# Dense layer with Mish on one core: x tiles 0 and 1 loaded as two, k 0 of w1 as two, and the first block multiplied in another order

## The chip, the core and the metric

The kernel runs on one core of one Trainium2 chip. A core has TensorE (PE), which multiplies and writes to PSUM; VectorE (DVE), ScalarE (ACT) and GpSimd (POOL), which work element by element; and SyncE (SP), which here only issues DMAs. Each engine takes its own instructions in order and waits for the others by semaphores. The metric is the device time of one execution in microseconds, as the median of several runs.

## The reference

x is 2048 x 512 (one batch), w1 512 x 1792, b1 1792 long, w2 1792 x 512, all bf16.

```python
def reference(x, w1, b1, w2):
    h = jnp.einsum("bsd,df->bsf", x, w1) + b1
    sp = jnp.log1p(jnp.exp(-jnp.abs(h))) + jnp.where(h > 0, h, jnp.zeros_like(h))
    act = h * jnp.tanh(sp)
    return jnp.einsum("bsf,fd->bsd", act, w2)
```

The function between the two products is Mish.

## The kernel before

The contraction over D = 512 has four k tiles of 128, F = 1792 has fourteen f tiles of 128, and S = 2048 is cut into four blocks of 512 rows, each of four row tiles of 128. A block takes two stages. In the first (line 180) each of its fourteen f tiles gets four matmuls, one for each k, with w1 as the weights and the transposed x (xT) as the moving operand, 512 columns wide; they add up in one of the eight PSUM banks. ScalarE reads the bank, adds the bias, applies Mish and writes bf16 to a_sb (line 163). In the second stage (line 202) each row tile gets fourteen matmuls, one for each f, with a_sb as the weights and w2 as the moving operand; VectorE copies the result to o_sb (line 208) and SP stores it. The fourteen f of a block take 56 matmuls of 512 columns, and so does its second stage.

x is needed transposed. Blocks 1 to 3 and row tiles 2 and 3 of block 0 are transposed by DMA. Row tiles 0 and 1 come as they are (x_nat) and are transposed by TensorE: sixteen small matmuls against an identity (line 147), each of half a tile's rows, into PSUM, from where VectorE and ScalarE copy them to xT (line 155). Until x_nat is there, TensorE runs a fill of matmuls on constants (line 105, WARM), whose results nobody reads.

Nothing schedules this program: the order of every engine is the order in which the code is written, and a wait is on the instruction that first needs it. The DMAs stand in two queues. ACT's queue gets k 0 and k 2 of w1 for f tiles 0 to 7. SP's queue gets x_nat, k 1, then, behind a wait for the third fill matmul, the DMA transpose of tiles 2 and 3, then k 3, the bias, the rest of w1 (f 8 to 13, all k), w2, and the transposes of blocks 1 to 3.

In block 0 the eight f tiles 0 to 7 are open at once, one PSUM bank each, and the calls of `first(fs, js, ks)` walk over them by k and by row tile: a call issues for every k and f one matmul over the row tiles js. The banks of f 0 to 7 are also those that the transposes of x used (line 147), so the first matmul into a bank waits until its transposes have been copied out. Each row tile is one fourth of a bank's columns, so a matmul over one tile has 128 columns, over two 256, over four 512. With the last k of an f its Mish is issued. f tiles 8 to 13 follow one by one with 512 columns (`mm1`).

## Time and profile before

| | us | |
|---|---|---|
| median of 3 runs | 105.19 | 105.11 to 105.49 |
| span of the profiled execution | 102.9 | first to last instruction |
| TensorE busy | 100.2 | 97% of the span |
| ScalarE busy | 39.5 | 38% |
| VectorE busy | 13.1 | 13% |
| chain: line 180 and line 202 | | 47% each |
| chain: the fill, line 105 | | 3% |

For the profiled execution the page gives the span alone. The median is 2.3 us above it; what lies outside the span (before the first instruction and after the last) is in no row.

How to read what follows. Times in a row are microseconds from the start of the span, engines as above; PEld is TensorE's loading of weights, which runs beside its matmuls, and SPq or ACTq an instruction that issues a DMA on that engine. A row of the timeline has the start, how long it lasted, engine, line, operation, what is written from what, the shape and how many were merged; in brackets the idle time before it and who ended it. Matmuls are pipelined: the time of one reaches into the next, so a pace is read from starts, not from durations. In rows the weights w1 and w2 are both called w_sb, and b1_sb is b_sb.

### The profile page before, as it was taken

To read this page: it belongs to the slowest core of one execution; us is meant where nothing else is said; L and a number is where in the kernel's file an instruction comes from. 1 tells how busy PE (TensorE), PEld (TensorE's weight loads), DVE (VectorE), ACT (ScalarE), POOL (GpSimd) and SP (SyncE) were. 2 spreads that over 40 slices of the span, in tenths; PEclk is the share of its full clock that TensorE was granted. 3 is DMA by queue.
4 is the path that set the end of the run, shared out by engine and by line. 5 is a ranking of instruction groups with operands and counts; after the bars stand their busy time and mean duration, and the time that the engine had idled before them with its cause. 6 is when DMAs were issued, how large, how long until landed. Compare 5 with 4: busy or idle time off the path is not lost.

```text
span 102.9 us, 1196 instructions
## 1 busy us (share of the span) xinstructions
PE 100.2 (97%) x527; PEld 48.8 (47%) x527; DVE 13.1 (13%) x26; ACT 39.5 (38%) x61; POOL 0.4 (0%) x5
## 2 busy tenths in 40 slices
PE   6999999999999999999999999999999999999993
PEld 2697444444444444444444444444444444444472
DVE  1203000220220000022220000022201000020241
ACT  4301999000047777000017777400006777700000
POOL 1000000000000000000000000000000000000000
DMA  2999999991110000011001000001111000001112
GB/s 61 375 283 358 363 243 112 269 237 51 51 51 0 0 6 0 0 51 51 20 31 51 0 0 10 0 3 48 51 51 51 0 0 0 0 6 51 51 51 51
DMA packets 12977, 7.94 MB, mean 77 GB/s; under 512 B 7980, under 2 KB 12332, under 8 KB 12972
## 3 DMA queue, kind: packets, MB, share of 16 engines
q1 hardware_dynamic: 12540, 7.33, 27.4%
q10 hardware_dynamic: 432, 0.54, 1.5%
q8 instruction: 4, 0.07, 0.3%
q14 instruction: 1, 0.01, 0.0%
HBM read 3.94 MB, written 2.10 MB: 59 GB/s over the span
## 4 chain that ended last, share of the span: by engine, by line
PE 97%; DVE 0%; ACT 0%; issue 0%
PE ps L180 47%; PE ps L202 47%; PE ps L105 3%; DVE xT L155 0%; ACT o_sb L232 0%; PE ps L147 0%
## 5 line engine op out<-in xcount | busy, mean ns | idle before, releaser
L163 ACT ACTIVATE a_sb<-ps,b_sb 128x512 bf16<-128x512 f32 x56 | 37.1, 698 | 47.9 <-PE ps L180 47.9
L180 PE MATMUL ps<-xT,w_sb 128*128 128x512 bf16 (+2 forms) x252 | 49.1, 355 | 0.2 <-DVE xT L155 0.2
L202 PE MATMUL ps<-w_sb,a_sb 128*128 128x512 bf16 (+3 forms) x252 | 49.1, 355 | 0.0
L180 PEld LDWEIGHTS ps<-xT,w_sb 128*128 128x128 bf16 x252 | 24.2, 98 | 24.1 <-DVE xT L155 0.3
L202 PEld LDWEIGHTS ps<-w_sb,a_sb 128*128 128x128 bf16 x252 | 23.2, 98 | 25.5
L208 DVE CAST o_sb<-ps 128x512 bf16<-128x512 f32 x15 | 10.4, 692 | 79.8 <-PE ps L202 79.8
L232 ACT ACTIVATE o_sb<-ps 128x64 bf16<-128x64 f32 x1 | 0.2, 224 | 11.5 <-PE ps L202 11.5
L105 PE MATMUL ps<-const-bfloat16-1.0 128*128 128x512 bf16 (+1 forms) x7 | 2.7, 566 | 0.8 <-PEq L289 0.8
L105 PEld LDWEIGHTS ps<-const-bfloat16-1.0 128*128 128x128 bf16 x7 | 0.9, 138 | 2.1 <-issue 2.1
L155 ACT ACTIVATE xT<-ps 128x256 bf16<-128x256 f32 (+1 forms) x3 | 0.9, 347 | 1.7 <-PE ps L147 1.7
L107 ACT ACT_TABLE_LOAD x1 | 1.3, 1283 | 0.7 <-PEq L289 0.7
L250 DVE STREAM_TRANSPOSE b_T<-b_nat 32x32 bf16<-32x32 bf16 x4 | 0.8, 202 | 3.3 <-DMA b_nat<-in_b_dram 3.2
L232 DVE CAST o_sb<-ps 128x320 bf16<-128x320 f32 (+1 forms) x2 | 0.8, 392 | 1.5 <-PE ps L202 1.5
L155 DVE CAST xT<-ps 128x128 bf16<-128x128 f32 (+1 forms) x2 | 0.6, 354 | 2.4 <-PE ps L147 2.4
L147 PEld LDWEIGHTS ps<-ident,x_nat 64*128 64x128 bf16 x16 | 0.4, 118 | 0.4 <-DMA x_nat<-in_x_dram 0.4
L147 PE MATMUL ps<-ident,x_nat 64*128 64x64 bf16 x16 | 0.5, 222 | 0.0
L130 DVE TENSOR_SCALAR ident<-diff 128x128 bf16<-128x128 int32 x1 | 0.2, 227 | 0.2 <-POOL diff L128 0.2
L128 POOL IOTA diff<- 128x128 int32 x1 | 0.2, 234 | 0.4 <-POOLq L289 0.4
L102 DVE MEMSET b_nat<- 32x64 uint32 x1 | 0.1, 112 | 0.8 <-PEq L289 0.8
L252 DVE CAST b_sb<-b_T 128x14 f32<-128x14 bf16 x1 | 0.2, 176 | 0.0
L289 POOL MEMSET const-bfloat16-1.0<- 128x1 bf16 x1 | 0.1, 102 | 0.0
L289 POOL MEMSET const-uint8-127<- 128x1 uint8 x1 | 0.1, 102 | 0.0
(2 smaller groups left out, 0.2 us busy)
## 6 DMA issues: line engine op xcount, KB each, us to landing
out_dram<-o_sb SPq DMA_DIRECT2D x15, 128.0 KB, 1.7
w_sb<-in_w_dram SPq DMA_DIRECT2D x1, 1792.0 KB, 10.7
w_sb<-in_w_dram SPq DMA_DIRECT2D x1, 768.0 KB, 6.1
w_sb<-in_w_dram ACTq DMA_DIRECT2D x2, 256.0 KB, 3.7
w_sb<-in_w_dram SPq DMA_DIRECT2D x2, 256.0 KB, 3.7
x_nat<-in_x_dram SPq DMA_DIRECT2D x1, 256.0 KB, 2.6
out_dram<-o_sb SPq DMA_DIRECT2D x1, 80.0 KB, 1.6
xT<-in_x_dram SPq DMA_TRANSPOSE x4, 5.0
```

Of the source, the lines that this page charges most:

```text
L105: t_fill = [pe.mark(nc.tensor.matmul(ps[:, 7, 0:n], c_w, c_m[:, 0:n], start=True, stop=True)) for n in WARM]
L107: act.eng.preload_act_table(ACT.Mish)
L128: t_diff = pool.mark(pool.eng.iota(diff[:, :], pattern=[[1, P]], base=0, channel_multiplier=-1))
L130: t_id = dve.mark(nc.vector.tensor_scalar(ident[:, :], diff[:, :], 0, None, ALU.is_equal))
L147: mm = nc.tensor.matmul(ps[:, b0 + h, lo:lo + H], x_nat[g, j, k * P:(k + 1) * P], ident[g, g], start=True, stop=True)
L155: t = eng.mark(nc.vector.tensor_copy(dst, src) if eng is dve else act.eng.activation(dst, src, ACT.Copy))
L163: t = act.mark(act.eng.activation(a_sb[:, f, starts[s]:starts[s + 1]], ps[:, bank, 0:n], ACT.Mish, bias=b1_sb[:, f:f + 1]))
L180: return nc.tensor.matmul(ps[:, bank, lo:hi], w1_sb[:, k, f * P:(f + 1) * P], xT[:, k, starts[s] + lo:starts[s] + hi], start=first, stop=( ...
L202: return nc.tensor.matmul(ps[:, bank, 0:hi - lo], a_sb[:, f, i * P:(i + 1) * P], w2_sb[:, f, lo:hi], start=(f == 0), stop=(f == FT - 1))
L208: t = dve.mark(nc.vector.tensor_copy(o_sb[:, i, lo:hi], ps[:, bank, 0:hi - lo]))
L232: t = eng.mark(nc.vector.tensor_copy(dst, src) if eng is dve else act.eng.activation(dst, src, ACT.Copy))
L250: t = dve.mark(nc.vector.transpose(b1_T[j * SQ:(j + 1) * SQ, :], b1_nat[:, j * SQ:(j + 1) * SQ]))
```

## The change

- Row tiles 0 and 1 of x are loaded as two DMAs of 128 KB, each with a semaphore of its own, a tile's 128 consecutive rows over the 128 partitions. Before, partition p held rows 2p and 2p + 1, and the output rows of the first two tiles were written back in that order; now they are written tile by tile.
- k 0 of w1 for f 0 to 7 comes as two DMAs of 128 KB, f 0 to 3 and f 4 to 7.
- k 3 of w1 stands ahead of the DMA transpose in SP's queue, and the transpose waits for the fourth fill matmul instead of the third.
- The fill has one 256-column matmul less.
- The transposes go tile by tile: for tile i its k 0 first, copied by VectorE, then k 1 to 3, copied by ScalarE in one instruction of 3 x 128 columns. Tile 0 uses banks 0, 1, 4, 5 and tile 1 banks 2, 3, 6, 7.
- In block 0, tiles 0 and 1 take all four k of f 0 to 7 first, with k 1 of f 0 to 3 ahead of k 0 of f 4 to 7; then tiles 2 and 3 take all four k of one f after the other, each with its Mish behind it.

```diff
-WARM = (512,) * 5 + (256,) * 2
+WARM = (512,) * 5 + (256,)
+HALF = 4
...
-        for k in (0, 2):
-            load_part(act, k, k + 1, 0, OPEN)
-        t_xn = load(sp, x_nat[:, :, :], x2[0:2 * P, :].rearrange("(p j) d -> p j d", p=P), "s_xn")
+        load_part(act, 0, 1, 0, HALF)
+        load_part(act, 0, 1, HALF, OPEN)
+        load_part(act, 2, 3, 0, OPEN)
+        t_xn = [load(sp, x_nat[:, i, :], x2[i * P:(i + 1) * P, :], "s_xn%d" % i) for i in range(2)]
         load_part(sp, 1, 2, 0, OPEN)
-        sp.wait(t_fill[2])
+        load_part(sp, 3, 4, 0, OPEN)
+        sp.wait(t_fill[3])
         t_x23 = load(sp, xT[:, :, 2 * P:4 * P], x2[2 * P:4 * P, :], "s_x23", True)
-        load_part(sp, 3, 4, 0, OPEN)
...
-            pe.wait(t_xn, t_id)
             H = P // 2
-            for b0, eng, js, ks in ((0, dve, (0,), (0,)), (2, act, (1,), (0,)), (4, dve, (0, 1), (1,)), (6, act, (0, 1), (2, 3))):
...
+            pe.wait(t_id)
+            for i in (0, 1):
+                pe.wait(t_xn[i])
+                for eng, b0, ks in ((dve, 2 * i, (0,)), (act, 4 + 2 * i, (1, 2, 3))):
...
+                    dst = xT[:, ks[0]:ks[-1] + 1, i * P:(i + 1) * P].rearrange("p k (h t) -> p k h t", h=2)
+                    src = ps[:, b0:b0 + 2, 0:m * H].rearrange("p h (k t) -> p k h t", k=m)
...
-            if i < 2:
-                return out2[0:2 * P, :].rearrange("(p j) d -> p j d", p=P)[:, i, :]
             return out2[i * P:(i + 1) * P, :]
...
-        first(range(4), (0,), (0,))
-        first(range(4), (1,), (0,))
-        first(range(4, OPEN), (0, 1), (0,))
-        first(range(OPEN), (0, 1), (1, 2))
-        first(range(OPEN), (2, 3), (0, 1, 2))
-        first(range(OPEN), None, (3,), True)
+        first(range(HALF), (0,), (0,))
+        first(range(HALF), (1,), (0,))
+        first(range(HALF), (0, 1), (1,))
+        first(range(HALF, OPEN), (0, 1), (0, 1))
+        first(range(OPEN), (0, 1), (2, 3))
+        for f in range(OPEN):
+            first((f,), (2, 3), range(KT), True)
```

TensorE's order from the transposes to the wait for tiles 2 and 3, before. c_dve and c_act are VectorE's and ScalarE's semaphores, s_xn the load of x_nat, s_w1_1_0 the load of k 1 from f 0 on, s_x23 the DMA transpose of tiles 2 and 3.

```order
L147 MATMUL ps<-ident,x_nat 128x64 [waits c_dve,s_xn]
L147 MATMUL ps<-ident,x_nat 128x64 x15
L180 MATMUL ps<-xT,w_sb 128x128 [waits s_w1_0_0,c_dve]
L180 MATMUL ps<-xT,w_sb 128x128
L180 MATMUL ps<-xT,w_sb 128x128 [waits c_act]
L180 MATMUL ps<-xT,w_sb 128x128 x5
L180 MATMUL ps<-xT,w_sb 128x256 [waits c_dve]
L180 MATMUL ps<-xT,w_sb 128x256
L180 MATMUL ps<-xT,w_sb 128x256 [waits c_act]
L180 MATMUL ps<-xT,w_sb 128x256
L180 MATMUL ps<-xT,w_sb 128x256 [waits s_w1_1_0]
```

And TensorE in the changed program at the same place, where s_xn0 and s_xn1 are the loads of tiles 0 and 1 and s_w1_0_4 that of the second half of k 0.

```order
L149 MATMUL ps<-ident,x_nat 128x64 [waits s_xn0,c_dve]
L149 MATMUL ps<-ident,x_nat 128x64 x7
L149 MATMUL ps<-ident,x_nat 128x64 [waits s_xn1]
L149 MATMUL ps<-ident,x_nat 128x64 x7
L181 MATMUL ps<-xT,w_sb 128x128 [waits s_w1_0_0,c_dve]
L181 MATMUL ps<-xT,w_sb 128x128
L181 MATMUL ps<-xT,w_sb 128x128 [waits c_dve]
L181 MATMUL ps<-xT,w_sb 128x128 x5
L181 MATMUL ps<-xT,w_sb 128x256 [waits c_act,s_w1_1_0]
L181 MATMUL ps<-xT,w_sb 128x256 x3
L181 MATMUL ps<-xT,w_sb 128x256 [waits s_w1_0_4]
```

The wait for k 1 moved from behind eight 128-column and four 256-column matmuls to behind the eight alone, and tile 1's transposes, with a wait of their own, stand ahead of the first matmul of line 181. The third 128-column matmul, into bank 2, waits for VectorE's copy of tile 1 where it waited for ScalarE's.

SP's queue at its start, before:

```order
L85 DMA x_nat<-in_x_dram 128x1024 [waits barrier_Pool_Activation_PE_DVE_SP_release]
L85 DMA w_sb<-in_w_dram 128x1024
L85 DMA_TRANSPOSE xT<-in_x_dram 128x4x256 [waits c_pe]
L85 DMA w_sb<-in_w_dram 128x1024
L85 DMA b_nat<-in_b_dram 14x128 [waits c_dve]
```

and SP's queue in the changed program:

```order
L86 DMA x_nat<-in_x_dram 128x512 [waits barrier_Pool_Activation_PE_DVE_SP_release]
L86 DMA x_nat<-in_x_dram 128x512
L86 DMA w_sb<-in_w_dram 128x1024 x2
L86 DMA_TRANSPOSE xT<-in_x_dram 128x4x256 [waits c_pe]
L86 DMA b_nat<-in_b_dram 14x128 [waits c_dve]
```

One DMA more stands ahead of k 1, and k 3 moved from behind the DMA transpose to ahead of it.

More of the change, by code (lines that the diff above doesn't have):

```diff
@@ L136, in transpose_x @@
         def transpose_x():
-            pe.wait(t_xn, t_id)
             H = P // 2
-            for b0, eng, js, ks in ((0, dve, (0,), (0,)), (2, act, (1,), (0,)), (4, dve, (0, 1), (1,)), (6, act, (0, 1), (2, 3))):
-                m = len(js)
-                for i, k in enumerate(ks):
-                    for n, j in enumerate(js):
-                        lo = (i * m + n) * H
+            pe.wait(t_id)
+            for i in (0, 1):
+                pe.wait(t_xn[i])
+                for eng, b0, ks in ((dve, 2 * i, (0,)), (act, 4 + 2 * i, (1, 2, 3))):
+                    m = len(ks)
+                    for n, k in enumerate(ks):
                         for h in (0, 1):
                             g = slice(h * H, (h + 1) * H)
-                            mm = nc.tensor.matmul(ps[:, b0 + h, lo:lo + H], x_nat[g, j, k * P:(k + 1) * P], ident[g, g],
-                                                  start=True, stop=True)
-                eng.wait(pe.mark(mm))
-                for i, k in enumerate(ks):
-                    dst = xT[:, k, js[0] * P:(js[-1] + 1) * P].rearrange("p (j h t) -> p j h t", j=m, h=2)
-                    src = ps[:, b0:b0 + 2, i * m * H:(i + 1) * m * H].rearrange("p h (j t) -> p j h t", j=m)
+                            mm = nc.tensor.matmul(ps[:, b0 + h, n * H:(n + 1) * H], x_nat[g, i, k * P:(k + 1) * P],
+                                                  ident[g, g], start=True, stop=True)
+                    eng.wait(pe.mark(mm))
+                    dst = xT[:, ks[0]:ks[-1] + 1, i * P:(i + 1) * P].rearrange("p k (h t) -> p k h t", h=2)
+                    src = ps[:, b0:b0 + 2, 0:m * H].rearrange("p h (k t) -> p k h t", k=m)
                     if m == 1:
@@ L155, in transpose_x @@
                     t = eng.mark(nc.vector.tensor_copy(dst, src) if eng is dve else act.eng.activation(dst, src, ACT.Copy))
-                    for j in js:
-                        t_cp[j, k] = t
-                free[b0] = free[b0 + 1] = [t]
+                    for k in ks:
+                        t_cp[i, k] = t
+                    free[b0] = free[b0 + 1] = [t]
         def mish(s, f, bank, t_mm):
```

## The prediction

> **What bounds the kernel now.** I read the chain of waits first, in order of time:
>
> ```profile
> 0.73 0.04 issue
> 0.77 2.72 PE ps L105 x7
> 3.49 0.19 PE ps L147 x3
> 3.68 0.02 issue
> 3.70 0.30 DVE xT L155
> 4.00 0.12 issue
> 4.13 12.32 PE ps L180 x84
> 16.45 12.09 PE ps L202 x56
> ```
>
> From 4.13 us on TensorE alone sets the time: every later piece is a run of matmuls that follows the one before without a gap. So the time can change in only three ways: by when the first matmul of line 180 starts, by gaps inside the first stage, and by the matmuls' own number and width. Their pace comes from the starts in the PE timeline, asked at narrow stretches:
>
> ```profile
> 4.13 0.22 PE L180 MATMUL ps<-xT,w_sb 128*128 128x128 bf16 x1 [0.17 <-DVE xT L155]
> ...
> 4.57 0.49 PE L180 MATMUL ps<-xT,w_sb 128*128 128x256 bf16 x3
> 5.01 0.49 PE L180 MATMUL ps<-xT,w_sb 128*128 128x256 bf16 x3
> 4.79 4.75 PE L180 MATMUL ps<-xT,w_sb 128*128 128x256 bf16 x42
> ...
> 16.28 0.38 PE L202 MATMUL ps<-w_sb,a_sb 128*128 128x512 bf16 x1
> ```
>
> Eight 128-column matmuls take 4.13 to 4.57, 0.055 us each. Four 256-column ones take 4.57 to 5.01, and 42 of them end 4.75 us after the first started: less the last one's own 0.27 that is 41 steps of 0.109. A 512-column one takes 12.09 / 56 = 0.216 (chain). Check: 5.01 + 40 x 0.1093 + 32 x 0.2159 = 16.29, and the second stage starts at 16.28. **The first stage has no gap once it runs**; at 5.01 it turns to k 1. The question is when the changed program gets there, and with how much work left.
>
> **The loads.** When they are issued (SP and ACT timelines), and how long until they land (the DMA view, asked around each issue):
>
> ```profile
> 0.74 0.40 SPq L85 DMA_DIRECT2D x_nat<-in_x_dram  x1
> ...
> 0.95 0.86 ACTq L85 DMA_DIRECT2D w_sb<-in_w_dram  x2
> ...
> 1.19 0.42 SPq L85 DMA_DIRECT2D w_sb<-in_w_dram  x1
> 2.24 1.31 SPq L85 DMA_TRANSPOSE xT<-in_x_dram  x1
> 3.60 0.57 SPq L85 DMA_DIRECT2D w_sb<-in_w_dram  x1
> 4.73 0.95 SPq L85 DMA_DIRECT2D w_sb<-in_w_dram  x2
> ...
> x_nat<-in_x_dram SPq DMA_DIRECT2D x1, 256.0 KB, 2.6
> w_sb<-in_w_dram ACTq DMA_DIRECT2D x1, 256.0 KB, 3.0
> w_sb<-in_w_dram ACTq DMA_DIRECT2D x2, 256.0 KB, 3.7
> w_sb<-in_w_dram SPq DMA_DIRECT2D x1, 256.0 KB, 3.6
> xT<-in_x_dram SPq DMA_TRANSPOSE x1, 4.4
> w_sb<-in_w_dram SPq DMA_DIRECT2D x1, 256.0 KB, 3.7
> w_sb<-in_w_dram SPq DMA_DIRECT2D x1, 768.0 KB, 6.1
> ```
>
> So x lands at 0.74 + 2.6 = 3.34, w1 k 0 at 3.95, k 1 at 1.19 + 3.6 = 4.79, x tiles 2-3 at 6.64, k 3 at 7.30, the rest of w1 at 10.83. ACT's two have a median of 3.7 and the first took 3.0, so k 2 (issued about 1.36) took some 4.4 and lands at about 5.8. The queue rows of three short stretches (2.45-2.70, 3.05-3.35, 3.65-3.95) show in what order the bytes move, q1 being SP's queue and q10 ACT's:
>
> ```profile
> q1 hardware_dynamic: 45, 0.09, 94.5%
> ...
> q10 hardware_dynamic: 56, 0.11, 98.4%
> ...
> q1 hardware_dynamic: 56, 0.11, 102.8%
> ```
>
> x alone, then k 0 alone, then k 1 alone: loads are served one after another in the order of issue, whichever queue they stand in. In the changed program that order is x0 (SP, 0.74), k 0 first half (ACT, 0.95), x1 (SP, about 1.19), k 0 second half (ACT, 1.36), k 1 (SP, about 1.64), k 2, k 3, x tiles 2-3. **Ahead of the end of k 1 stand the same 768 KB as before**, and no split can bring it forward.
>
> What the split costs is the rate. The windows view, whose last number is GB/s:
>
> ```profile
> 1.75:2.40 0.65, 0.65 (x3) 0.15 (x1) 0.00 (x0) 0.27 (x1) 0.00 (x0) 1.00 0.91 154
> 2.50:4.50 2.00, 1.83 (x27) 1.05 (x26) 0.62 (x2) 0.74 (x3) 0.00 (x0) 1.00 1.04 391
> 11.00:13.00 2.00, 2.00 (x11) 0.87 (x9) 0.00 (x0) 2.00 (x5) 0.00 (x0) 1.00 1.08 356
> ```
>
> Rows of 2048 bytes move at 391 GB/s (2.5 to 4.5); w2, with rows of 1024 bytes, at 356 (11 to 13). The 512 KB of x and k 0 now go in rows of 1024 bytes: 1.47 us for 1.34, so +0.13. The slow start (154 GB/s, 100 KB by 2.40) is either of bytes or of pieces; in the second case pieces of half the size leave 50 KB more to do, another 0.13. I take the first, as the rate is the only part that a row shows, and keep the second for the range.
>
> Landings after: x0 at 3.34 - 0.34 + 0.03 = 3.03; the first half of k 0 at 3.40; x1 at 3.95 - 0.37 + 0.10 = 3.68; the second half at 4.08; **k 1 at 4.79 + 0.13 = 4.92**.
>
> **TensorE's path after.** How long a landed x takes until it is multiplied:
>
> ```profile
> 3.42 0.13 PEld L147 LDWEIGHTS ps<-ident,x_nat 64*128 64x128 bf16 x4 [0.41 <-DMA x_nat<-in_x_dram]
> 3.70 0.29 DVE L155 CAST xT<-ps 128x128 bf16<-128x128 f32 x1 [2.38 <-PE ps L147]
> 4.10 0.18 PEld L180 LDWEIGHTS ps<-xT,w_sb 128*128 128x128 bf16 x3 [0.26 <-DVE xT L155]
> L155 ACT ACTIVATE xT<-ps x3: 278/378/384, 3.8 to 4.3; 128x256 bf16<-128x256 f32 x2, 128x128 bf16<-128x128 f32 x1
> L147 PEld LDWEIGHTS ps<-ident,x_nat x16: 95/124/129, 3.4 to 3.7; 64*128 64x128 bf16 x16
> ```
>
> Landing to weights 0.08, to the cast 0.36, to the matmul 4.13 - 3.34 = 0.79.
>
> - The fill is a 256-column matmul shorter and ends about 3.07; x0's transposes wait for x0 until 3.11, so that edit is hidden.
> - TensorE takes its instructions in order, so x1's transposes stand ahead of the first matmul: they wait until 3.76 and are through by about 3.96 (sixteen took 0.4, eight 0.2). The first matmul starts at about 3.99, where it was 4.13: 0.14 earlier.
> - Only f 0 and 1 can run: banks 2 and 3 held x1's transposes and are free with x1's VectorE cast, at 3.68 + 0.79 = 4.47. Six 128-column matmuls follow, to 4.80.
> - ACT now casts k 1-3 of a tile at once, 384 columns. 128 took 0.278 and 256 took 0.381, so 0.484 by the slope; the ends are 0.381 and 0.765, a narrower and two separate ones. After x1: 0.08, eight transposes and their end 0.4, the cast 0.48, 0.1 to the matmul: 3.68 + 1.07 = 4.75, at worst 5.03.
> - The next matmul is of k 1, which lands at 4.92 and is ready 0.11 later (0.08 as above, 0.03 from weights to matmul): **5.03**. This wait ends last. The four f of the second half of k 0 are queued behind it, though their weights are there.
>
> Now the work. Before, 40 of 256 and 32 of 512 columns were left at 5.01. After, only the eight 128-column matmuls are done, and 60 of 256 and 24 of 512 are left: 6.56 + 5.18 = 11.74. The first stage ends at 5.03 + 11.74 = 16.77 instead of 16.28, **+0.49 us**. Of it 0.44 is the work that before hid the wait for k 1 (four 256-column matmuls moved behind it), 0.02 that sixteen 256-column matmuls replace eight of 512, 0.02 the later turn to k 1; the rest is rounding.
>
> Later waits are covered. k 2 is wanted at 5.03 + 1.32 = 6.35 and lands at 5.9; k 3 at 7.22, and with it now ahead of the transpose it lands about 5.9 + 0.67 = 6.6. x tiles 2-3 are wanted at 8.10; everything up to k 3 landed at 7.30 before, so 7.43 after is its bound, a cover of 0.7. Each 0.1 beyond that costs 0.1. The rest of w1 is wanted at 8.10 + 32 x 0.109 = 11.6, against 10.96. SP's wait moves from the third to the fourth fill, 0.43 later, but two loads that stood behind the transpose are now one, so what follows on SP is issued no later. The bias and Mish:
>
> ```profile
> 8.44 0.18 DVE L252 CAST b_sb<-b_T 128x14 f32<-128x14 bf16 x1
> 9.86 8.21 ACT L163 ACTIVATE a_sb<-ps,b_sb 128x512 bf16<-128x512 f32 x14 [5.20 <-PE ps L180]
> ```
>
> The bias is ready at 8.62 (after: about 8.8), the first f is complete at 8.7, so Mish starts near 8.8 instead of 9.86. At 0.59 each it frees bank 0 by 9.4, wanted at 11.6. Nothing waits there, and the earlier Mish is worth nothing, as nothing waited for it before.
>
> **Sum.** Span 102.9 + 0.49 = 103.4. The median of the three runs, 105.19, is 2.3 above this span; the change touches nothing outside the span, so 105.19 + 0.49 = **105.68**, +0.47%. Less or more than 0.5% (0.53 us) is about what a measurement can tell from no change.
>
> **Rivals.**
> 1. *A quicker start of the loads.* If short pieces took none of the slow start, 0.65 us at 391 instead of 154 GB/s would be 154 KB, 0.39 us: k 1 ready at 4.64, x1's chain at 4.4. The stage then ends at 16.38, +0.10: 105.3. The slow stretch speaks for its possibility, nothing for its cause. Even this isn't faster; faster by 0.5% would need k 1 at 4.0.
> 2. *The other side: half pace for longer.* The fill's weight loads show TensorE at half its pace at first:
>
> ```profile
> 1.58 0.15 PEld L105 LDWEIGHTS ps<-const-bfloat16-1.0 128*128 128x128 bf16 x1 [0.28 <-issue]
> 2.01 0.15 PEld L105 LDWEIGHTS ps<-const-bfloat16-1.0 128*128 128x128 bf16 x1 [0.28 <-issue]
> ```
>
> 512 columns each 0.43, against 0.216 later. By 4.13 the pace is full, though the windows' clock column says 1.00 throughout and doesn't show the switch. It came after some 2.9 us of nearly unbroken work (0.77 to about 3.7). The changed program has 2.3 us of fill and then mostly waits until 5.03. If the switch needs such a stretch anew, counted from 4.1, it comes at 7.0, and half of 7.0 - 5.03 is lost: 0.49 + 1.0, 106.7. It decides if the switch has not come by 5.03. Against it: most of the stretch stays.
> 3. *x tiles 2-3 late, or k 1 later still.* The slow start by pieces and a late engine put k 1 at 5.2, or the transpose slips past 8.1 by 0.2: 105.9.
> 4. *The order isn't that of issue,* k 1 ahead of the second half of k 0. Then x1's chain decides, 4.75 to 5.03: 105.4 to 105.7, so it hardly matters.
>
> On rival 2 the Trainium skill, "TensorE: Matmul & The Clock Gate", Part 1, says that the full clock is granted after a busy window of about 3.4 us, and that the windows run freely, whatever the kernel does. By that rule the instant differs from run to run; an estimate with a window missed, the switch 3.4 us after 5.03, loses 1.7 us more, 107.4. The switch near 3.7, 2.9 us after the first matmul, agrees with a window that began before it.
>
> **How the numbers follow.** Forecast (k 1 ready at 4.9 to 5.15): 0.65, 105.5 to 105.85, about three fifths of it within 0.5%. Rivals 1 and 4: 0.11, all within. Rival 3: 0.09 slower. Rival 2: 0.12 slower. Faster, from what I don't see: 0.03. Together 0.50 the same and 0.47 slower. Range 105.2 to 106.3: it takes in rival 1 and rival 3 and leaves most of rival 2 out.
>
> **What would show it.** In the changed trace: first matmul of line 181 near 4.0; two waits among the first eight, then one for the weights of k 1, ended near 5.0; 256-column steps of 0.109 from there; no gap at x tiles 2-3; line 201 from about 16.8. Wrong if k 1 lands well before 4.8, if steps after 5.0 are 0.21, or if gaps stand later than that.

## The result, and the profile after

| | before | after |
|---|---|---|
| median, us | 105.15 (6 runs, 104.36 to 105.49) | 109.97 (6 runs, 109.74 to 110.36) |
| ratio | | 1.0487, 95% interval 1.0442 to 1.0533 |
| span of the profiled execution | 102.9 | 108.9 |
| first matmul of block 0 (line 180, now 181) | 4.13 | 4.03 |
| first matmul on k 1 | 5.01 | 7.83 |
| start of the second stage (line 202, now 201) | 16.28 | 22.31 |
| TensorE busy | 100.2 (97%) | 103.6 (95%) |

The change makes the kernel 4.9% slower, where +0.47% was forecast and 106.3 us was the upper end of the range. The profiled execution of after took 110.24 us for a span of 108.9. The same difference, 1.3 to 1.4 us, lies between time and span in the later runs of the kernel before (104.8 with 103.5, 105.34 with 104.0), so the profiled execution of before, with its 102.9, was one of about 104.2 to 104.3. The ratios here and below leave out executions more than 1.5% above the fastest of the same kernel, no ratio is given where only one is left, and the profiled executions of e1, f1, f6 and h5 are among those left out.

The chain of waits of after, in order of time:

```profile
0.74 0.39 SPq L86
1.13 0.06 issue
1.19 0.42 SPq L86
1.61 0.05 issue
1.66 6.12 DMA w_sb<-in_w_dram
7.78 0.05 issue
7.83 14.65 PE ps L181 x84
22.47 12.09 PE ps L201 x56
34.56 12.09 PE ps L181 x56
```

The fill and VectorE's cast have left the chain. In their place stands a load: k 1 of w1, issued at 1.66 and landed 6.12 later. From the start of the second stage on nothing has changed, 12.09 a stage. The whole loss lies ahead of 22.31, and it has two parts, which the PE timeline shows when it is asked at narrow stretches:

```profile
4.03 1.12 PE L181 MATMUL ps<-xT,w_sb 128*128 128x128 bf16 x8
7.83 0.39 PE L181 MATMUL ps<-xT,w_sb 128*128 128x256 bf16 x1 [2.67 <-DMA w_sb<-in_w_dram]
...
8.44 5.11 PE L181 MATMUL ps<-xT,w_sb 128*128 128x256 bf16 x23
...
13.74 2.46 PE L181 MATMUL ps<-xT,w_sb 128*128 128x256 bf16 x21
...
22.31 0.38 PE L201 MATMUL ps<-w_sb,a_sb 128*128 128x512 bf16 x1
```

First part: the eight 128-column matmuls run from 4.03, and the next one waits for k 1 until 7.83. Second part: after the gap 23 matmuls of 256 columns take 5.11; less the last one's own 0.42 that is 22 steps of 0.213, half the pace. From 13.53 on, 21 take 2.46; less 0.27 that is 20 steps of 0.109, full pace. The sum: the turn to k 1 came at 7.83 instead of the forecast 5.03, **+2.80**. With 11.74 of work left the stage would have ended at 19.57; it ended at 22.31, **+2.74** for half pace until 13.53. With the 0.49 that were forecast this makes 6.03, which is 22.31 - 16.28.

The half pace does not begin behind the gap. Two more rows, of the 128-column matmuls ahead of it:

```profile
4.33 0.72 PE L181 MATMUL ps<-xT,w_sb 128*128 128x128 bf16 x5
...
4.84 0.31 PE L181 MATMUL ps<-xT,w_sb 128*128 128x128 bf16 x1
```

From the one at 4.33 to the last at 4.84 there are five steps in 0.51, 0.10 each, where before has 0.055. So in this execution TensorE had not come to full pace yet when it began to wait for k 1; it came to it only at 13.53.

How long each load took from issue to landing (the DMA view, asked around each issue; they were issued at 0.74, 0.95, 1.19, 1.35, 1.66, 1.84, 2.12 and the transpose of tiles 2 and 3 at 2.67):

```profile
x_nat<-in_x_dram SPq DMA_DIRECT2D x1, 128.0 KB, 2.2
w_sb<-in_w_dram ACTq DMA_DIRECT2D x1, 128.0 KB, 2.4
x_nat<-in_x_dram SPq DMA_DIRECT2D x1, 128.0 KB, 2.5
w_sb<-in_w_dram ACTq DMA_DIRECT2D x1, 128.0 KB, 5.2
w_sb<-in_w_dram SPq DMA_DIRECT2D x1, 256.0 KB, 6.1
w_sb<-in_w_dram ACTq DMA_DIRECT2D x1, 256.0 KB, 6.6
w_sb<-in_w_dram SPq DMA_DIRECT2D x1, 256.0 KB, 6.5
xT<-in_x_dram SPq DMA_TRANSPOSE x1, 6.9
```

And the windows view of after over the same time (the last three numbers are the granted clock, the share of time that the DMA engines had packets, and GB/s):

```profile
2.50:3.20 0.70, 0.70 (x3) 0.08 (x1) 0.00 (x0) 0.00 (x0) 0.00 (x0) 1.00 1.14 359
3.20:4.20 1.00, 0.90 (x19) 0.61 (x18) 0.51 (x2) 0.55 (x2) 0.00 (x0) 1.00 0.63 146
4.20:5.80 1.60, 0.95 (x8) 0.56 (x6) 0.07 (x1) 0.43 (x1) 0.00 (x0) 1.00 0.77 212
5.80:8.20 2.40, 0.37 (x2) 0.28 (x3) 0.00 (x0) 0.00 (x0) 0.00 (x0) 1.00 1.20 225
8.60:11.00 2.40, 2.40 (x14) 1.66 (x11) 0.98 (x5) 0.00 (x0) 0.00 (x0) 1.00 1.09 344
```

The first three loads come as forecast, at 359 GB/s. Then, from 3.2 to 5.8, only 146 and 212 GB/s move, and the engines hold packets for 0.63 and 0.77 of the time, although four loads are queued: part of the engines' time is idle while some loads are behind. The row from 5.8 to 8.2 says less, because the DMA transpose of tiles 2 and 3 runs in it with its small packets. Here are the packets of after in that stretch (DMA view), and the windows row of before for a stretch with its own transpose:

```profile
DMA packets 732, 0.54 MB, mean 225 GB/s; under 512 B 527, under 2 KB 531, under 8 KB 732
```

```profile
5.00:7.00 2.00, 2.00 (x21) 1.79 (x19) 0.00 (x0) 0.00 (x0) 0.00 (x0) 1.00 1.19 288
```

With the transpose the even loads of before, too, come down to 288 GB/s at a share of 1.19, so the row of after mixes two causes. From 8.6 on the rate is back. Here is the table of landings, forecast and measured:

| | x0 | k 0, first half | x1 | k 0, second half | k 1 | k 2 | k 3 | tiles 2-3 |
|---|---|---|---|---|---|---|---|---|
| forecast | 3.03 | 3.40 | 3.68 | 4.08 | 4.92 | 5.9 | 6.6 | 7.43 at most |
| after | 2.94 | 3.33 | 3.66 | 6.59 | 7.78 | 8.40 | 8.60 | 9.53 |

Each load raises its semaphore in 16 steps, as many as the core has DMA engines, and the trace has the time of each. I take a step as the landing of one engine's part; the trace doesn't name the engine. In before the parts of k 1 land from 4.45 to 4.83; in after from 4.80 to 7.78, and half of those of the second half of k 0 are there by 4.02 while the last comes at 6.59. Some parts are in time and others fall behind by up to 3 us; a load is there when its last part is.

### The profile page after: what moved, and what is told of

Read it like the earlier page. It is cut to its first block, busy times and chain, and to the rows that moved or that the text cites. A ratio compares the mean times of both kernels' runs of the same rounds, so it can differ in the third digit from the quotient of the medians.

```text
span 108.9 us, 1212 instructions
## 1 busy us (share of the span) xinstructions
PE 103.6 (95%) x534; PEld 51.1 (47%) x534; DVE 13.1 (12%) x26; ACT 39.9 (37%) x60; POOL 0.4 (0%) x5
## 3 DMA queue, kind: packets, MB, share of 16 engines
HBM read 3.94 MB, written 2.10 MB: 55 GB/s over the span
## 4 chain that ended last, share of the span: by engine, by line
PE 91%; DMA 6%; SPq 1%; issue 0%; ACT 0%
PE ps L181 47%; PE ps L201 44%; DMA w_sb<-in_w_dram 6%; SPq L86 1%; ACT o_sb L231 0%
## 5 line engine op out<-in xcount | busy, mean ns | idle before, releaser
L181 PE MATMUL ps<-xT,w_sb 128*128 128x512 bf16 (+2 forms) x260 | 52.5, 367 | 2.7 <-DMA w_sb<-in_w_dram 2.7
L181 PEld LDWEIGHTS ps<-xT,w_sb 128*128 128x128 bf16 x260 | 26.7, 104 | 27.6 <-DMA w_sb<-in_w_dram 2.9
L156 ACT ACTIVATE xT<-ps 128x384 bf16<-128x384 f32 x2 | 1.0, 491 | 1.6 <-PE ps L149 1.6
L156 DVE CAST xT<-ps 128x128 bf16<-128x128 f32 x2 | 0.6, 291 | 2.4 <-PE ps L149 2.4
```

The costliest lines, as they stand in the source:

```text
L156: t = eng.mark(nc.vector.tensor_copy(dst, src) if eng is dve else act.eng.activation(dst, src, ACT.Copy))
L181: return nc.tensor.matmul(ps[:, bank, lo:hi], w1_sb[:, k, f * P:(f + 1) * P], xT[:, k, starts[s] + lo:starts[s] + hi], start=first, stop=( ...
```

## The experiments

Two questions were open: what slows the loads from the fourth on, and whether the half pace is a result of the gap or something of its own. "Before" in a heading or a diff means that the edit was made to the kernel before, all others to the changed kernel. The letters in the expectations stand for theories: A that what was moved ahead or behind (the transpose by DMA, k 3) slows the loads, B that the gap brings the half pace, G that it is the two queues, H that it is the number of loads in flight; the rest is said in words at each run. Ratios are against runs of the kernel before on the same chip, whose median in the four groups was 104.67, 104.59, 104.91 and 105.08. Landings and steps are those of each run's one profiled execution.

### k 3, the transpose, and the pace

**e1_k3_behind**: k 3 goes back behind the transpose of tiles 2 and 3.

```diff
         load_part(sp, 1, 2, 0, OPEN)
-        load_part(sp, 3, 4, 0, OPEN)
         sp.wait(t_fill[3])
         t_x23 = load(sp, xT[:, :, 2 * P:4 * P], x2[2 * P:4 * P, :], "s_x23", True)
+        load_part(sp, 3, 4, 0, OPEN)
```

> The changed kernel with one thing undone: k 3 of w1 stands behind the DMA transpose again (the transpose still waits for the fourth fill matmul). Theory A, that a DMA transpose issued right behind whole loads (0.11 us after the last one in the changed kernel, 0.43 us in the kernel before) takes away the service of the loads still on their way: the last load before it on SP now ends 0.6 us earlier, k 1 lands near 4.9 instead of 7.78, and the time falls to 105.5 to 107.5, the upper end if the half pace of TensorE lasts. Rival A2, that the halves themselves (seven loads for four, 1024-byte rows) slow the loads: k 1 still lands after 7, time 109 to 110. Rival A3, that three whole k loads at once slow each other: like A here.

Measured: 108.18 us, ratio 1.0326 (1.0267 to 1.0384); the profiled execution was the longest of the four, 109.88. The second half of k 0 lands at 5.80, k 1 at 7.38. With both splits in, k 3's new place isn't needed to make the loads late. The time is 0.8 us below what was expected if the halves are at fault; why, this run doesn't show.

**e2_x23_after_k1**: the transpose isn't issued until k 1 has landed.

```diff
-        sp.wait(t_fill[3])
+        sp.wait(t_w1[1, 0])
```

> The changed kernel with the DMA transpose held until k 1 of w1 has landed, instead of until the fourth fill matmul; k 3 stays ahead of it and the halves stay. Theory A: with no transpose issued while k 0, k 1 and k 2 are on their way, loads run at some 350 GB/s, k 1 lands near 4.9, tiles 2 and 3 near 7.5 to 8, time 105.5 to 107.5. Rivals A2 (the halves) and A3 (three whole loads at once): k 1 lands after 7 as in the changed kernel, the transpose later still, time 110 or more.

Measured: 108.15 us, 1.0329 (1.0277 to 1.0381). The transpose's row in the SP timeline, then k 1's row in the DMA view, then two rows of the windows view, all of this run:

```profile
7.11 1.30 SPq L86 DMA_TRANSPOSE xT<-in_x_dram  x1
```

```profile
w_sb<-in_w_dram SPq DMA_DIRECT2D x1, 256.0 KB, 5.4
```

```profile
3.30:5.30 2.00, 1.44 (x24) 0.85 (x24) 0.58 (x2) 0.98 (x2) 0.00 (x0) 1.00 0.74 174
5.30:7.10 1.80, 0.00 (x0) 0.00 (x0) 0.00 (x0) 0.00 (x0) 0.00 (x0) 1.00 0.72 278
```

No transpose is in flight before 7.11, and the loads are served at 174 GB/s all the same; k 1, issued at 1.66, lands at 7.09. Theory A falls: with both splits in, the transpose isn't needed for it. The pace can be read on both sides of the gap (4.64 to 7.14): 128-column steps of 0.058 ahead of it, then full pace up to 7.58, steps of 0.211 for 256 columns to 10.96, and full pace from there. In this run the clock column of the windows view (the third number from the end) shows the stretch as well:

```profile
7.60:10.90 3.30, 3.30 (x18) 2.30 (x16) 0.46 (x3) 0.00 (x0) 0.00 (x0) 0.50 0.56 107
```

**e3_before_k3_first** (before): k 3 ahead of the transpose, and nothing else.

```diff
         load_part(sp, 1, 2, 0, OPEN)
+        load_part(sp, 3, 4, 0, OPEN)
         sp.wait(t_fill[2])
         t_x23 = load(sp, xT[:, :, 2 * P:4 * P], x2[2 * P:4 * P, :], "s_x23", True)
-        load_part(sp, 3, 4, 0, OPEN)
```

> The kernel before with one thing of the change: k 3 of w1 ahead of the DMA transpose, which is then issued about 0.1 us behind a whole load. Theory A and rival A3: k 1 and k 2 land microseconds late although x and k 0 are whole, TensorE gets gaps inside the first stage, 107 to 110. Rival A2 (the halves): no gap, 105 to 105.5.

Measured: 105.24 us, 1.0035 (1.0003 to 1.0067). k 1 lands at 4.74, k 2 at 5.40, k 3 at 6.19; from 2.5 to 4.5 the rate is 390 GB/s. Five whole loads one behind the other are served as the prediction assumed.

**e4_fill_gap**: seven 512-column matmuls on constants into the free bank 7, behind the eight 128-column ones, so that TensorE has work while it waits for k 1. Nobody reads their results.

```diff
         first(range(HALF), (1,), (0,))
+        pe.wait(*free[7])
+        for _ in range(7):
+            nc.tensor.matmul(ps[:, 7, 0:512], c_w, c_m[:, 0:512], start=True, stop=True)
         first(range(HALF), (0, 1), (1,))
```

> The changed kernel with seven more 512-column fill matmuls (no result used) behind the eight first matmuls, where TensorE otherwise idles from 4.95 to 7.83. Theory B, that TensorE runs at half pace until 13.4 because it idled: k 1 still starts near 7.8 to 8.0, but its 256-column matmuls then step 0.109 instead of 0.213, and the time falls by some 2.5 us to about 107.4. Rival, that the slow steps come from the loads' traffic or from the order of the matmuls: steps of 0.21 remain and the time stays at 110.

Measured: 106.82 us, 1.0192 (1.0121 to 1.0264). The PE timeline of this run:

```profile
4.25 0.51 PE L181 MATMUL ps<-xT,w_sb 128*128 128x128 bf16 x6
...
4.60 1.69 PE L259 MATMUL ps<-const-bfloat16-1.0 128*128 128x512 bf16 x7
...
7.04 9.31 PE L181 MATMUL ps<-xT,w_sb 128*128 128x256 bf16 x71 [0.75 <-DMA w_sb<-in_w_dram]
...
7.81 2.89 PE L181 MATMUL ps<-xT,w_sb 128*128 128x256 bf16 x25
```

k 1 is still late (7.04 for the first matmul), but 25 matmuls take 2.89; less 0.27 that is 24 steps of 0.109, full pace. Its span is 105.4, and 102.9 + 0.49 + (7.04 - 5.03) = 105.4: with the gap filled the half pace is gone, and only the wait is left. But the fill didn't bring the full pace, it kept it: six 128-column matmuls ahead of the fill take 0.51, and less the last one's 0.22 that is five steps of 0.058. The run to compare with is e2, where the pace was full ahead of the gap too, the gap stayed empty, and half pace followed. In that sense theory B holds: the empty gap took the full pace away, and the filled one kept it. In after, where full pace hadn't come when the gap began, the gap put off its coming; no trace shows such a gap filled, but all four executions of e4 took 107.14 or less, and the shortest of after 109.74.

### Which split, and is it the two queues

**f1_before_x_split** (before): x as two loads of 128 KB, both waited for together; all else as before.

```diff
-        t_xn = load(sp, x_nat[:, :, :], x2[0:2 * P, :].rearrange("(p j) d -> p j d", p=P), "s_xn")
+        t_xn = [load(sp, x_nat[:, i, :], x2[0:2 * P, :].rearrange("(p j) d -> p j d", p=P)[:, i, :], "s_xn%d" % i) for i in range(2)]
...
-            pe.wait(t_xn, t_id)
+            pe.wait(*t_xn, t_id)
```

> The kernel before with one thing of the change: x tiles 0 and 1 as two DMAs of 128 KB (1024-byte rows), waited for together. The transpose is ruled out by the run that held it (k 1 landed at 7.1 all the same) and k 3's place by the kernel before with k 3 first. Theory D, that one more load on SP's queue ahead of k 1 is enough to slow the loads behind: k 1 lands after 5.5, a gap at k 1, 106 or more. Theory E, that 1024-byte rows of w1's k 0 are what slows it: no gap, 104.5 to 105.3. Theory F, that three loads ahead of a load on ACT's queue slow it: no gap either.

Measured: 106.74 us (4 runs, 104.85 to 107.42, no ratio). x lands at 2.95 and 4.19, k 0 at 3.87, k 2 at 5.09, k 1 at 5.79: the second half of x now stands behind k 0, and k 1 is issued behind k 2. The loads go at an even 340 GB/s (2.5 to 5.5). The loss of this execution is another than in the changed kernel: TensorE waits for the later x and is at half pace until 8.94. The shortest of the four, at 104.85, can hardly have had it.

**f2_before_k0_cols** (before): k 0 as two loads by columns, f 0 to 3 and f 4 to 7.

```diff
-        for k in (0, 2):
-            load_part(act, k, k + 1, 0, OPEN)
+        load_part(act, 0, 1, 0, 4)
+        load_part(act, 0, 1, 4, OPEN)
+        load_part(act, 2, 3, 0, OPEN)
```

> The kernel before with one thing of the change: k 0 of w1 as two DMAs of 128 KB by columns (1024-byte rows at w1's pitch of 3584 bytes), x whole. Theories E and F: k 1 and k 2 land microseconds late, 106 or more. Theory D: no gap, 104.5 to 105.3.

Measured: 104.81 us, 1.0018 (0.9986 to 1.005). x lands at 3.44, k 0 at 3.75 and 4.92, k 1 in between at 4.56. TensorE waits 0.32 for the second half and loses nothing else. This split alone does no harm.

**f6_before_k0_parts** (before): k 0 as two loads of 64 partitions, so with whole rows of 2048 bytes.

```diff
-        for k in (0, 2):
-            load_part(act, k, k + 1, 0, OPEN)
+        t_k0 = [load(act, w1_sb[h * 64:(h + 1) * 64, 0, 0:OPEN * P], w1v[h * 64:(h + 1) * 64, 0, 0:OPEN * P], "s_k0_%d" % h) for h in (0, 1)]
+        for f in range(OPEN):
+            t_w1[0, f] = t_k0[0]
+        load_part(act, 2, 3, 0, OPEN)
...
+            if k == 0 and f < OPEN:
+                pe.wait(t_k0[1])
```

> The kernel before with k 0 of w1 as two DMAs of 128 KB by partitions (64 rows of 2048 bytes each), so the same number of loads and bytes as the split by columns, but no shorter rows. Theory E (row length): no gap, 104.5 to 105.3. Theory F (number of loads on ACT's queue): as late as the split by columns, 106 or more.

Measured: 108.04 us (4 runs, 106.01 to 108.2, no ratio). The halves land at 4.41 and 6.31, k 1 at 5.20. It was to show whether short rows are at fault; long rows on half the partitions are worse than short rows on all (6.31 for 4.92 in f2). As this cut has a slowness of its own, the run doesn't tell what short rows do; f2, where short rows did no harm, does.

**f3_all_on_sp**: the seven loads in the same order, all on SP.

```diff
-        load_part(act, 0, 1, 0, HALF)
-        load_part(act, 0, 1, HALF, OPEN)
-        load_part(act, 2, 3, 0, OPEN)
-        t_xn = [load(sp, x_nat[:, i, :], x2[i * P:(i + 1) * P, :], "s_xn%d" % i) for i in range(2)]
+        t_xn = [load(sp, x_nat[:, 0, :], x2[0:P, :], "s_xn0")]
+        load_part(sp, 0, 1, 0, HALF)
+        t_xn.append(load(sp, x_nat[:, 1, :], x2[P:2 * P, :], "s_xn1"))
+        load_part(sp, 0, 1, HALF, OPEN)
         load_part(sp, 1, 2, 0, OPEN)
+        load_part(sp, 2, 3, 0, OPEN)
         load_part(sp, 3, 4, 0, OPEN)
```

> The changed kernel with the seven first loads in the same order, all on SP's queue, none on ACT's. If the slow service comes from two queues that are served side by side (theory G), k 1 lands near 5.0 and the time falls to 105.5 to 107.5. If it comes from the short rows or the number of loads (D, E), k 1 still lands after 7, 109 to 110.

Measured: 108.46 us, 1.0359 (1.0291 to 1.0428). The second half of k 0 lands at 5.05, k 1 at 6.37, k 2 at 7.42, with 239 GB/s from 2.5 to 4.0 and 273 from 4 to 6. The rates say little here, since SP issues one 128 KB load per 0.46 us, which alone is some 280 GB/s by these numbers. The parts say more: half of those of k 1 are there by 5.30, the last at 6.37. So one queue doesn't mend it and two queues aren't needed for it; theory G, with 5.0 for k 1, falls. It is milder, though: k 1 isn't after 7 as the others expected, and its last part is 1.1 behind the median instead of 1.4. The Trainium skill, "DMA: Bandwidth & Descriptors", section "Issuing engines are not separate DMA queues", says that DMAs of different engines share the same 16 DMA engines, so that a second issuing engine saves issue time only. On the issue time this run agrees, with k 1 issued at 2.59 instead of 1.66; as the parts lie less far apart than in after, it doesn't show that the queues make no other difference.

**g1_before_both** (before): both splits, f1 and f2 together, and nothing else of the change.

```diff
-        for k in (0, 2):
-            load_part(act, k, k + 1, 0, OPEN)
-        t_xn = load(sp, x_nat[:, :, :], x2[0:2 * P, :].rearrange("(p j) d -> p j d", p=P), "s_xn")
+        load_part(act, 0, 1, 0, 4)
+        load_part(act, 0, 1, 4, OPEN)
+        load_part(act, 2, 3, 0, OPEN)
+        t_xn = [load(sp, x_nat[:, i, :], x2[0:2 * P, :].rearrange("(p j) d -> p j d", p=P)[:, i, :], "s_xn%d" % i) for i in range(2)]
...
-            pe.wait(t_xn, t_id)
+            pe.wait(*t_xn, t_id)
```

> The kernel before with both splits of the loads and nothing else of the change (x as two, k 0 by columns as two; orders of matmuls and transposes as before; k 3 behind the transpose). Each split alone left k 1 in time. Theory H, that the service falls to about half once six or more loads are on their way at once (the kernel before has four ahead of the transpose, each single split and k 3 first have five): six now, so k 1 and k 2 land after 6.5, a gap, and 106.5 to 109. Rival: the splits are harmless together too and another part of the change (the tiles' rows, k 3, the later transpose) does it: k 1 near 5.2, no gap over 0.6, 105 to 106.

Measured: 106.57 us, 1.0163 (1.0083 to 1.0243). k 1 lands at 6.28, but half of its parts by 5.03: the same picture as in the changed kernel, milder. The two splits alone make k 1 late. The time lost here is another thing: TensorE waits for the second half of x until 4.21 and is at half pace until 9.47, so that k 1 is there before it is wanted, and there is no gap at it.

### How many loads, in which order

**g2_hold_k2_k3**: k 2, k 3 and the transpose are held until the second half of k 0 has landed. Five loads are in flight, as in e3.

```diff
-        load_part(act, 2, 3, 0, OPEN)
...
         load_part(sp, 1, 2, 0, OPEN)
+        sp.wait(t_w1[0, HALF])
+        load_part(sp, 2, 3, 0, OPEN)
         load_part(sp, 3, 4, 0, OPEN)
-        sp.wait(t_fill[3])
```

> The changed kernel with k 2 and k 3 of w1 (both on SP) and the transpose issued only when the second half of k 0 has landed, so that no more than five loads are on their way at once; both splits stay. Theory H: k 1 lands at 4.9 to 5.2, the gap ahead of it shrinks from 3.0 to under 0.7 us, 105.3 to 106.5 (k 2, held until about 4.3, may cost 0.2 more). Rival E2, that 512 KB in 1024-byte rows are what slows the loads behind: k 1 still after 6.5, 108 or more.

Measured: 107.45 us, 1.0267 (1.0219 to 1.0314). The second half of k 0 and k 1 in the DMA view of this run, issued at 1.37 and 1.66, and two rows of its windows:

```profile
w_sb<-in_w_dram ACTq DMA_DIRECT2D x1, 128.0 KB, 4.0
w_sb<-in_w_dram SPq DMA_DIRECT2D x1, 256.0 KB, 3.9
```

```profile
2.50:3.20 0.70, 0.70 (x3) 0.08 (x1) 0.00 (x0) 0.00 (x0) 0.00 (x0) 1.00 1.13 381
3.20:5.20 2.00, 1.82 (x25) 1.17 (x24) 0.58 (x2) 0.98 (x2) 0.00 (x0) 1.00 0.63 183
```

With five loads the service breaks at the same place, 381 GB/s and then 183. Half of the parts of the second half of k 0 are there by 3.94 and the last at 5.35. Theory H, with k 1 at 4.9 to 5.2, falls: the number in flight alone isn't it. Its rival, with k 1 after 6.5, isn't met either. k 1 comes 2.3 us earlier than in after, and 1.5 earlier than in e4, which has the loads of after: more loads behind make it later.

**g3_no_splits**: the changed kernel with x and k 0 whole. Order of multiplication, fill, transposes and k 3's place stay changed.

```diff
-        load_part(act, 0, 1, 0, HALF)
-        load_part(act, 0, 1, HALF, OPEN)
+        load_part(act, 0, 1, 0, OPEN)
...
-        t_xn = [load(sp, x_nat[:, i, :], x2[i * P:(i + 1) * P, :], "s_xn%d" % i) for i in range(2)]
+        t_xn = [load(sp, x_nat[:, :, :], x2[0:2 * P, :].rearrange("(p j) d -> p j d", p=P), "s_xn")] * 2
...
+            if i < 2:
+                return out2[0:2 * P, :].rearrange("(p j) d -> p j d", p=P)[:, i, :]
             return out2[i * P:(i + 1) * P, :]
```

> The changed kernel without its two splits: x as one load of 2048-byte rows, k 0 as one, everything else as changed (k 3 ahead of the transpose, its wait, the transposes tile by tile, the order of the matmuls). Five loads. Theory H and E2: no slow service, k 1 lands near 4.8, TensorE turns to it at 4.9 to 5.0 with 11.74 us left, so 0.3 to 0.5 above the kernel before: 104.9 to 105.6. If another part of the change slows the loads: 107 or more.

Measured: 105.41 us, 1.0043 (1.0002 to 1.0084). k 1 in its DMA view (issued at 1.19), its windows, and the end of its first stage:

```profile
w_sb<-in_w_dram SPq DMA_DIRECT2D x1, 256.0 KB, 3.5
```

```profile
2.50:4.50 2.00, 1.73 (x23) 0.84 (x22) 0.51 (x2) 0.54 (x2) 0.00 (x0) 1.00 1.03 388
```

```profile
16.87 0.38 PE L202 MATMUL ps<-w_sb,a_sb 128*128 128x512 bf16 x1
```

388 GB/s, k 1 at 4.74, the second stage from 16.87. That is 0.59 later than before, where the prediction's sum for the changed program was 0.49. Without the splits the rest of the change costs about what the prediction said, +0.4%. (Its eight 128-column matmuls are partly at half pace, so TensorE turns to k 1 at 4.98, after it was ready, and the first step there is still 0.213.)

**g4_split_k2_k3** (before): k 3 first, and k 2 and k 3 each as two loads by columns. Seven loads, four of them halves, but behind the whole ones.

```diff
-        for k in (0, 2):
-            load_part(act, k, k + 1, 0, OPEN)
+        load_part(act, 0, 1, 0, OPEN)
+        load_part(act, 2, 3, 0, 4)
+        load_part(act, 2, 3, 4, OPEN)
...
+        load_part(sp, 3, 4, 0, 4)
+        load_part(sp, 3, 4, 4, OPEN)
         sp.wait(t_fill[2])
         t_x23 = load(sp, xT[:, :, 2 * P:4 * P], x2[2 * P:4 * P, :], "s_x23", True)
-        load_part(sp, 3, 4, 0, OPEN)
```

> The kernel before with k 3 ahead of the transpose (which alone cost 0.35%) and, besides, k 2 and k 3 each as two loads by columns; x, k 0 and k 1 are whole and stand first. Seven loads, as in the changed kernel, but the halves are behind k 1. Theory H: the service falls for k 1 as well, it lands after 5.5, a gap at k 1, 106 or more. Rival E2 (short rows ahead) or that only what is queued behind many loads suffers: k 1 lands near 4.7, no gap there, and k 2 or k 3 may be late, 105 to 106.5.

Measured: 105.19 us, 1.0056 (1.0025 to 1.0087). Its windows:

```profile
2.50:5.50 3.00, 2.68 (x35) 1.76 (x34) 0.62 (x2) 0.90 (x3) 0.00 (x0) 1.00 1.03 373
```

k 1 lands at 4.88, the first halves at 5.26 and 5.60, the others at 6.74 and 6.95. Seven loads, and four short ones among them, are served at 373 GB/s when the short ones stand last; only the third half has a part that is 0.9 behind (half of its parts by 5.88, the last at 6.74). What the changed kernel has, and none of the even runs with as many loads, is short loads at the front with whole ones behind.

### Which of the two splits, and what stands behind them

**h3_k0_whole**: the changed kernel with k 0 whole, x still as two.

```diff
-        load_part(act, 0, 1, 0, HALF)
-        load_part(act, 0, 1, HALF, OPEN)
+        load_part(act, 0, 1, 0, OPEN)
```

> The changed kernel with k 0 whole again (x split, all else as changed), so six loads in the order x0, k 0, x1, k 2, k 1, k 3. Theory J, that it is the four short loads one behind the other at the front that break the even service of the 16 engines, after which whole loads come slowly too: two short loads with a whole one between them keep it even, k 2 lands near 5.0 and k 1 near 5.7 (only by its place in the order), the spread of one load's landings stays under 0.5, 105.5 to 107 (the later end by the half pace). Rival, that each split costs by itself in the changed kernel: k 1 after 6.5 with a spread over 1.

Measured: 108.62 us, 1.0314 (1.0234 to 1.0394). x lands at 2.75 and 4.04, k 0 at 3.74; then k 2 at 6.72, with half of its parts by 4.79, and k 1 at 6.92. Theory J falls: undoing k 0's split alone hardly helps, and what breaks from the fourth load on is now a whole load.

**h4_x_whole**: the changed kernel with x whole, k 0 still as two.

```diff
-        t_xn = [load(sp, x_nat[:, i, :], x2[i * P:(i + 1) * P, :], "s_xn%d" % i) for i in range(2)]
+        t_xn = [load(sp, x_nat[:, :, :], x2[0:2 * P, :].rearrange("(p j) d -> p j d", p=P), "s_xn")] * 2
...
+            if i < 2:
+                return out2[0:2 * P, :].rearrange("(p j) d -> p j d", p=P)[:, i, :]
             return out2[i * P:(i + 1) * P, :]
```

> The changed kernel with x whole again (k 0 split, all else as changed), six loads in the order x, k 0 first half, k 1, k 0 second half, k 2, k 3. Theory J: k 1 lands near 4.6, spreads under 0.5, 104.7 to 105.8. Rival, that each split costs by itself: k 1 after 5.5, 106 or more.

Measured: median 106.01 us of ten runs, 104.83 to 107.59; ratio 1.0047 (1.0001 to 1.0094). Its windows:

```profile
2.50:4.50 2.00, 1.55 (x21) 0.70 (x19) 0.51 (x2) 0.35 (x1) 0.00 (x0) 1.00 1.01 352
5.00:7.00 2.00, 2.00 (x16) 1.44 (x13) 0.00 (x0) 0.02 (x1) 0.00 (x0) 1.00 1.19 226
```

k 1 is there at 4.59, the second half of k 0 at 4.92. Here too the parts come apart, but only behind these: k 3 lands at 7.67, with half of its parts by 5.51, and k 2 at 7.92. (The 226 GB/s of the second row are no proof of it, as the transpose runs there; before has 288 in that stretch.) So theory J's spreads under 0.5 aren't met, though k 1 is where it put it. What TensorE needs first is in time, and the split of x carries most of the loss.

**h5_k1_first**: g2 with k 1 issued ahead of the four halves.

```diff
+        load_part(sp, 1, 2, 0, OPEN)
         t_xn = [load(sp, x_nat[:, i, :], x2[i * P:(i + 1) * P, :], "s_xn%d" % i) for i in range(2)]
-        load_part(sp, 1, 2, 0, OPEN)
+        sp.wait(t_w1[0, HALF])
+        load_part(sp, 2, 3, 0, OPEN)
         load_part(sp, 3, 4, 0, OPEN)
-        sp.wait(t_fill[3])
```

> The run with k 2, k 3 and the transpose held (k 1 landed at 5.5 there, second half of k 0 at 5.35), with k 1 as the first load of all: k 1 whole, then the four halves. Same loads, same bytes, another order. Theory J: with a whole load ahead the halves are served evenly, all five landed by 5.1 with spreads under 0.5; the time isn't the point (x comes 0.7 later). Rival K, that four halves are slow wherever they stand: the last half lands after 5.3 with a spread over 1.

Measured: 108.45 and 106.84 us, no ratio; the time says little, as x comes last. k 1 in its DMA view:

```profile
w_sb<-in_w_dram SPq DMA_DIRECT2D x1, 256.0 KB, 3.2
```

k 1 lands at 3.91, the halves at 4.25, 4.67, 4.94 and 5.26, one every 0.35 or so. The parts of each load lie 0.8 to 1.0 apart, from the first load to the last, where g2 has 1.6 for the second half of k 0 and h6 below at most 0.4. That is between theory J (all by 5.1, under 0.5) and rival K (after 5.3, over 1): with the whole load first the lag doesn't grow from load to load, but the service isn't even, and the last landing is only 0.26 ahead of g2's 5.52.

**h6_four_alone**: g2 with k 1 held too, so that nothing stands behind the four halves until they have landed.

```diff
+        sp.wait(t_w1[0, HALF])
         load_part(sp, 1, 2, 0, OPEN)
+        load_part(sp, 2, 3, 0, OPEN)
         load_part(sp, 3, 4, 0, OPEN)
-        sp.wait(t_fill[3])
```

> The same run with k 1 held too, so that the four halves are alone on their way until the last has landed. Rival K: the second half of k 0 lands after 5 with a spread over 1 though nothing stands behind it. Theory L, that the four are served evenly and only a load behind them, that moves on the engines that are done first, holds up the rest: all four land by 4.4 with spreads under 0.5. The time isn't the point (k 1 is issued after 4.2, so 107 or more).

Measured: 109.08 us (2 runs), 1.0395 (1.0299 to 1.049); k 1 is issued at 4.10 only and lands at 6.83. The second half of k 0, issued at 1.35, in its DMA view:

```profile
w_sb<-in_w_dram ACTq DMA_DIRECT2D x1, 128.0 KB, 2.7
```

The halves land at 3.06, 3.40, 3.81 and 4.08, within 0.13 us of what the prediction had, and the parts of each lie 0.3 to 0.4 apart: theory L. Alone, four halves do what the sum said. With one whole load behind them (g2) the fourth comes at 5.35, with three and a transpose (after) at 6.59.

### What the runs settle, and what they leave open

Settled, for both splits together: the late landings need the short loads (g3 with whole ones is even) and whole loads behind them (h6 without is even; h5, with the whole one first, is in between). They need neither the transpose (e2) nor k 3's place (e1, e3) nor two queues (f3), and the number of loads alone doesn't bring them about (g4 has seven, g2 five). Some of a load's 16 parts are hit and others not, mostly from the fourth or fifth load on (in f3, on one queue, a little from the second).

Not settled is what one split does. In the kernel before each split alone leaves the parts together (f1, f2: at most 0.6 apart up to k 1 and k 2); in the changed kernel each alone breaks them (h3 from the fourth load on, h4 from the fifth). The two halves of x are cut in another way in f1 than in h3 (alternate rows against consecutive ones), but f2 and h4 have the same cut of k 0. What differs in both pairs is k 3, behind the transpose in f1 and f2 and ahead of it in h3 and h4, the moment of the transpose, and what is multiplied when; which of these decides wasn't tried.

Open: what in a DMA engine makes its part wait. Other cuts, other spacings, and whole loads between all four halves weren't tried. Nor did any of these kernels come out faster than the kernel before; the nearest, f2, is 1.0018 with an interval on both sides of 1.

## Why the prediction was wrong

**What held.** The first three loads were served in the order of issue and landed within 0.1 of the forecast, at 359 GB/s for the 356 that it took for short rows. (Nearly all runs issue these loads on the two queues in turn, so that the two queues simply take turns would look the same.) The first matmul of line 181 started at 4.03 (3.99 was forecast). ACT's cast of 384 columns, forecast at 0.484 by the slope, is this group on the page of after:

```profile
L156 ACT ACTIVATE xT<-ps 128x384 bf16<-128x384 f32 x2 | 1.0, 491 | 1.6 <-PE ps L149 1.6
```

The turn to k 1 ended last of the early waits, as said, and the work left was 11.74. The chain runs from 7.83 to the second stage without a gap, so no later wait cost anything. That was luck and not the forecast cover: k 2 (8.40), k 3 (8.60) and tiles 2 and 3 (9.53) landed 1.4 to 2.1 us after the times at which the forecast wanted them (6.35, 7.22 and 8.10), and were in time only because k 1 held TensorE up for longer. The cost of the changed order, +0.49, is about what g3 shows once the splits are gone (16.87 for 16.28).

**What failed.** The step is "Landings after", and in it "the second half at 4.08; k 1 at 4.92". It took the bytes ahead of a load, divided them by a rate, and shifted the landings of before by the difference. The rate had been read from whole loads, one behind the other; the trace of before had no short loads with others queued behind. "Ahead of the end of k 1 stand the same 768 KB as before, and no split can bring it forward" was right as far as it goes, but the split can put it back. The allowance was 0.13 for the row length and another 0.13, in the range only, for the slow start; measured were +2.51 on the second half of k 0 and +2.86 on k 1. The prediction had a row that showed a much lower rate for these first loads, 154 GB/s in the slow start. At that rate the 256 KB of k 1 alone take 1.70 instead of 0.67 us. As a bound for loads of a kind that the trace doesn't show, it should have opened the range by one us at least before half pace.

**Rival 2 came true as a result of that.** Its mechanism, half pace for longer, was right in kind, and so was its condition, that the switch has not come by 5.03: the steps of 0.10 up to 4.84 show it. What stood against it, "most of the stretch stays", wasn't enough in this execution. Its size was 2.74 and not 1.0, since it was worked out for a turn to k 1 at 5.03 and a switch at 7.0. After a gap up to 7.83 the switch came at 13.53. Its chance of 0.12 was for a half pace without a long gap, and rival 3 had a late k 1 without half pace; the case in which the one brings the other wasn't there. e2 and e4 show that they are one chain: an empty gap was followed by half pace, a filled one wasn't.

**A small one.** The 2.3 us between the median and the span of before were taken to lie outside the span. It is 1.3 to 1.4, and the rest was that the profiled execution was one of the shorter. For the forecast this changes nothing, as the 0.49 were added to the median. What can make an execution longer by so much is seen in e3, whose loads are even: its pace is half up to 6.25 where before has full pace by 4.13, and its span is 103.9. That the longer executions of before are of this kind is likely, but none of them has a trace.

## What to carry to other kernels

A load's landing is a sum of bytes over GB/s only for a pattern of loads that a trace has shown; where a change puts short loads in front of a queue, look in its trace at the landings of every load behind them, last part and median, before anything else. A gap of 2 to 3 us in TensorE early in a kernel can cost itself and then as much again in half pace (2.80 and 2.74 here). Read the pace from the starts of equal matmuls on both sides of the gap: busy time doesn't show it, and the clock column showed it in e2, h3 and f6 but said 1.00 throughout in after. A fill of matmuls in such a gap can keep the pace (1.0487 became 1.0192; of the 3.5 us between the two profiled spans 0.79 come from an earlier k 1). It is better not to have the gap: with x whole (h4), or x and k 0 whole (g3), the ratio is 1.005 or less.
